# Staging the last x2 half of block 0 and the weight sums in the x region, and other queues and slots for loads and jobs

## The chip, the cores and the metric

One NeuronCore of one Trainium2 chip runs the kernel. The metric is the device time of one execution in microseconds (us). A profiled execution gives, beside its own time, the span from its first to its last recorded instruction, and the rows read below. TensorE is PE (its weight loads PEld), VectorE DVE, ScalarE ACT, GpSimd POOL and SyncE SP.

## What is computed

The reference chains a decaying causal attention and two feed-forward layers, over 8 x 576 = 4608 tokens and a width of 512:

```python
scores = scale * np.matmul(q, k.transpose(0, 1, 3, 2))
Dmat = np.where(rel >= 0, gamma[:, None, None] ** rel[None, :, :], 0.0)
x = np.matmul(scores * Dmat[None], v)          # to (4608, 512)
x2 = ((x @ w1) * (x @ w2)) @ w3 @ w_out        # d_ff 1024
h = x2 @ w_in                                  # d_ff 2048
out = (h * np.clip(h + 3.0, 0.0, 6.0) / 6.0) @ w_out2
```

The kernel multiplies in full precision by splitting each operand into a high and a low part (fp32r), with three matmuls for one product. It folds w3 @ w_out into one matrix W.

## The kernel before, in words

**Blocks.** The 4608 tokens are nine blocks (0 to 8) of 512. For each block PE computes, for the eight f-tiles of 128 of d_ff, `pa` = x @ w1 and `pb` = x @ w2 (lines 130 to 132, four tiles each of three matmuls for one k), then `px` = (a * b) @ W. Blocks 0 and 8 keep W whole in SBUF (`Wh`, `Wl`, `Wm`) and take `px` in 4 x 8 products of three matmuls. Blocks 1 to 7 take it in **seven products** of half size instead of eight (`px_str`, line 773: 168 matmuls of 256 columns): combinations of the halves of a * b (`pair`, `keep`) by combinations of the quarters of W, which stream from DRAM (`wsd`) through three buffers (`wb` in Wp's space, `st["w3"]` in the x region), 14 halves of 512 KB a block on SP (line 730). Four PSUM banks A to D gather the products; D is reused by the sixth product and C by the seventh, after VectorE's adds of line 748 have read them. Each block's result x2 is then turned into seven half-size operands as well (sums, high part, low part) and stored to DRAM (`xod`); so are the weights w_in (`wid`) and w_out2 (`wqd`), one "i" job and one "q" job in each of blocks 1 to 8 (`job`: load by SP at line 107, convert on ACT at line 155 and on DVE at lines 160 and 164, sums at line 861, high part at 864, low part at 135, store at 872; all in the one staging area `stg` and `stg_hi`). Stage 2 (h and the gate) and stage 3 (the last product) then read these operands back, with 896 to 1024 KB transfers; in stage 2, `stg` and `stg_hi` are the temporaries, and ACT's copy of line 1038 is the first step after a bank's first product.

**Attention in between.** At four places of a block PE makes an `excursion` (some 180 small matmuls, lines 214 and 251) that computes the attention of one 128-token tile t of a later block. It needs kv and qk of tile t+1, loaded by POOL (lines 193 and 198), and v scaled by DVE (`v_scale`, line 204).

**The order.** Everything is in program order per engine. `at(s, f)` puts a step at slot s, and each group of three large matmuls calls `tick()`, which emits the steps of the slot that is due:

```python
def at(s, f):
    slots.setdefault(max(s, now[0]), []).append(f)
def tick():
    q_ = slots.get(now[0], [])
    while q_:
        q_.pop(0)()
```

A slot thus sets where a step stands in its engine's row of instructions, not when it runs: an engine that is free runs ahead of PE, and a step that must wait holds up all that stand behind it on its engine. Block j begins at slot B0 + 96 j; its pa and pb take slots 0 to 63 and px slots 64 to 95.

**Around the end of block 0.** W's seven combinations are made from `Wh`, `Wl` and `Wm` by four weight jobs (`w_job`: sums at lines 593 and 597, high part on ACT at line 600, low part on DVE, two 512 KB stores at 607). They share two tiles in the space of block 0's x (`xh`, `xl`), so that a job's high part waits for the store before. Block 0's x2 comes out as px columns 0, 2, then 1, 3 (`x2_copy`, line 821): column 2 and column 3 are both copied into `stg[0:512]`, so that the copy of column 3 waits until the store of the first half (line 845) has read `stg`.

**Lines to follow.** 186 to 199 loads of qk and kv; 472 to 501 excursions and their loads; 587 to 617 weight jobs and the opening of the spaces that follow; 645 `a_copy` (frees the bank of pa); 673 to 693 the combinations of a * b in blocks 1 to 7; 738 to 764 the adds of px; 808 to 847 x2; 850 to 882 the i and q jobs; 936 to 947 the loads of the last block (`xop`, `wset`).

## Time and profile before

| | us |
|---|---|
| three runs, median (lowest to highest) | 1455.13 (1451.58 to 1455.41) |
| the profiled execution's own time | 1451.42 |
| its span | 1449.6 |
| PE busy | 1419.8 (98% of the span) |
| DVE busy | 1091.0 (75%) |
| ACT busy | 573.4 (40%) |
| POOL busy | 143.1 (10%) |
| mean DMA rate | 242 GB/s |

PE is busy but for 29.8 us. What is busy is no peak: a matmul at the lower of the clock's two levels counts as busy too. A saving can therefore come from PE's waits and from stretches at the lower clock, and each wait has a place, an engine that it waited for, and work that stood ahead on that engine. The span and the own time of the profiled execution differ by 1.8 us, which lies around the program.

### The profile page before, as it was taken

What the parts mean: (1) busy time and instruction counts of PE and PEld (TensorE: products, weight loads), DVE (VectorE), ACT (ScalarE), POOL (GpSimd) and SP (SyncE); (2) the same over time, 40 slices, a digit from 0 to 9 for tenths busy, and PEclk for the clock granted to TensorE, in tenths of its full rate; (3) what the DMA queues carried; (4) which work ended last, traced back from release to release, by engine and by line L of the source; (5) the groups of instructions that cost most, each with busy time, mean ns of one, the idle gap of its engine ahead of it and who ended that gap; (6) DMA issues with size and microseconds to landing.
All of it is one profiled execution on the core that took longest, in us unless ns stands there. A gap on an engine that the chain in (4) does not pass through costs nothing.

```text
span 1449.6 us, 28030 instructions
## 1 busy us (share of the span) xinstructions
PE 1419.8 (98%) x11315; PEld 1204.7 (83%) x11315; DVE 1091.0 (75%) x1880; ACT 573.4 (40%) x842; POOL 143.1 (10%) x329
## 2 busy tenths in 40 slices
PE   9999799999999999999799999999999999999999
PEld 4588688888888888889688898888888888888888
DVE  7888668786877777686436666665668899889897
ACT  7583334343434343333323343333334433433433
POOL 1101010100010101000002242221221000000000
PEclk9999899999999999999999999999999999999999
DMA  9775758787878787869999674645898444555441
GB/s 361 302 240 182 262 204 307 269 286 278 301 265 300 267 303 262 300 248 304 351 346 408 213 276 156 243 187 203 319 342 266 129 122 137 146 146 145 135 124 62
DMA packets 214658, 351.32 MB, mean 242 GB/s; under 512 B 11168, under 2 KB 144064, under 8 KB 210944
## 3 DMA queue, kind: packets, MB, share of 16 engines
q1 hardware_dynamic: 142432, 212.89, 43.1%
q0 software_dynamic: 21792, 73.72, 13.7%
q10 hardware_dynamic: 50304, 62.92, 12.3%
q8 instruction: 89, 1.46, 0.4%
q14 instruction: 41, 0.34, 0.1%
HBM read 231.51 MB, written 117.96 MB: 241 GB/s over the span
## 4 chain that ended last, share of the span: by engine, by line
PE 88%; DVE 6%; DMA 4%; ACT 1%; issue 1%; POOL 0%; ACTq 0%; DVEq 0%; POOLq 0%
PE pb L1299 16%; PE pb L130 12%; PE pb L132 12%; PE pb L131 12%; PE pb L1300 8%; PE px L773 6%; PE pa L130 4%; PE pa L131 4%; PE Wps L514 4%; PE pa L132 4%; PE z L251 2%; PE sc L214 2%; DMA wb<-wsd 1%; DMA xod<-wb 1%; DVE stg L135 1%; DVE pair L135 1%
## 5 line engine op out<-in xcount | busy, mean ns | idle before, releaser
L1299 PE MATMUL pb<-wq,op 128*128 128x512 f32 x1000 | 346.7, 391 | 0.0
L1300 PE MATMUL pb<-wq,op 128*128 128x256 f32 x1000 | 280.0, 280 | 0.0
L1299 PEld LDWEIGHTS pb<-wq,op 128*128 128x128 f32 x1000 | 187.0, 187 | 41.0
L130 PE MATMUL pb<-xop,wset 128*128 128x512 f32 (+1 forms) x558 | 205.3, 368 | 0.0
L131 PE MATMUL pb<-xop,wset 128*128 128x512 f32 (+1 forms) x558 | 205.2, 368 | 0.0
L132 PE MATMUL pb<-xop,wset 128*128 128x512 f32 (+1 forms) x558 | 205.2, 368 | 0.0
L1177 ACT CAST op<-unit 128x1024 fp32r<-128x1024 f32 x126 | 131.5, 1052 | 173.5 <-DVE unit L1163 152.8
L1300 PEld LDWEIGHTS pb<-wq,op 128*128 128x128 f32 x1000 | 189.0, 189 | 0.0
L135 DVE TENSOR_TENSOR op<-unit,op 128x1024 fp32r<-128x1024 f32 x126 | 154.0, 1222 | 30.5 <-ACT op L1177 30.5
L773 PE MATMUL px<-pair,wb 128*128 128x256 f32 x1176 | 147.6, 286 | 9.0 <-DVE x L748 4.8
L773 PEld LDWEIGHTS px<-pair,wb 128*128 128x128 f32 x1176 | 144.4, 193 | 11.6 <-issue 7.3
L132 PEld LDWEIGHTS pb<-xop,wset 128*128 128x128 f32 x558 | 105.2, 189 | 17.5
L131 PEld LDWEIGHTS pb<-xop,wset 128*128 128x128 f32 x558 | 105.2, 189 | 17.4
L130 PEld LDWEIGHTS pb<-xop,wset 128*128 128x128 f32 x558 | 105.2, 189 | 17.3
L130 PE MATMUL pa<-xh,w1h 128*128 128x512 f32 x280 | 111.3, 397 | 8.0 <-ACT a L645 8.0
L130 PE MATMUL pb<-xh,w2h 128*128 128x512 f32 x288 | 113.8, 395 | 0.0
L132 PE MATMUL pb<-xh,w2l 128*128 128x512 f32 x288 | 112.2, 390 | 0.0
L131 PE MATMUL pb<-xl,w2h 128*128 128x512 f32 x288 | 112.1, 389 | 0.0
L131 PE MATMUL pa<-xl,w1h 128*128 128x512 f32 x280 | 110.2, 394 | 0.0
L132 PE MATMUL pa<-xh,w1l 128*128 128x512 f32 x280 | 110.0, 393 | 0.0
L1163 DVE TENSOR_TENSOR unit<-unit 128x1024 f32<-128x1024 f32 x72 | 87.8, 1220 | 0.6
L684 ACT CAST pair<-sraw 128x512 fp32r<-128x512 f32 (+1 forms) x56 | 40.8, 728 | 95.6 <-DVE sraw L135 95.6
(204 smaller groups left out, 2231.6 us busy)
## 6 DMA issues: line engine op xcount, KB each, us to landing
wb<-wsd SPq DMA_DIRECT2D x98, 512.0 KB, 6.5
unit<-gd SPq DMA_DIRECT2D x72, 512.0 KB, 5.3
xop<-xod SPq DMA_DIRECT2D x28, 1024.0 KB, 7.7
xod<-wb ACTq DMA_DIRECT2D x28, 896.0 KB, 4.9
qk<-in_qk_dram POOLq DMA_DIRECT2D x36, 512.0 KB, 7.1
kv<-in_kv_dram POOLq DMA_DIRECT2D x32, 512.0 KB, 5.1
gd<-gw POOLq DMA_DIRECT2D x60, 256.0 KB, 2.7
gd<-g POOLq DMA_DIRECT2D x57, 256.0 KB, 3.7
```

Source lines behind the costliest of these rows:

```text
L130: nc.tensor.matmul(out=out_ap, lhsT=sh, rhs=mh, start=first, stop=False, **kw)
L131: nc.tensor.matmul(out=out_ap, lhsT=sh, rhs=ml, start=False, stop=False, **kw)
L132: nc.tensor.matmul(out=out_ap, lhsT=sl, rhs=mh, start=False, stop=last, **kw)
L135: eng.tensor_tensor(out=out_ap, in0=x, in1=y, op=ALU.subtract)
L214: nc.tensor.matmul(out=out_ap, lhsT=lhsT, rhs=rhs, start=True, stop=True, skip_group_check=True)
L514: nc.tensor.matmul(out=ps, lhsT=w3f[:, n // 4 % 8, n % 4 * 128:n % 4 * 128 + 128], rhs=wo[:, j, :], start=j == 0, stop=j == KF - 1)
L684: nc.scalar.copy(out=st["pair"][f % 4][:, 0, a:b], in_=st["raw"][:, a + 1:b + 1])
L773: nc.tensor.matmul(out=out_ap, lhsT=w[:, kk, x, ms], rhs=y, start=k not in seen, stop=kk == 3 and x == 1, skip_group_check=True)
L1163: nc.vector.tensor_tensor(out=f32_unit(o), in0=t[0], in1=t[1], op=f)
L1177: nc.scalar.copy(out=op_tiles(7 * b + p)[0], in_=src())
L1299: nc.tensor.matmul(out=c[k], lhsT=h[:, ts], rhs=w, start=first and kt == 0, stop=False, skip_group_check=True)
L1300: nc.tensor.matmul(out=c[k][:, 0:256], lhsT=l[:, ts], rhs=w[:, 0:256], start=False, stop=kt == 7, skip_group_check=True)
```

## The change

1. **x2 of block 0.** px columns 1 and 3 are copied into one new tile in the x region (`xl`), not into the pool `tmp` and into `stg`; the sums, high part, low part and store of that half come 11 slots later.
2. **Weight jobs.** Each of the four has one tile in turn (`xh`, `xl`, `xh`, `xl`) and keeps its high and low part in it; they stand at slots 65, 73, 97, 112 of block 0 (65, 73, 98, 106 before). `open_sw` comes 6 slots later.
3. **Late kv/qk loads.** The loads that follow the fourth excursion of blocks 1 to 6 (kv and qk for six tiles) are issued by SP, in its row behind the seven products' weights.
4. **Other slots.** The q jobs of blocks 1 to 7 load and convert 8 slots earlier and sum 4 slots later, with the store where it was; the first i job comes 8 slots later. In block 8 the i job comes 8 and the q job 16 slots later, the reload of `Wh` 6 slots later, and the `xop` loads 6 to 31 slots later (one stays).

```diff
-    def load_qk(t):
+    def load_qk(t, q=nc.gpsimd):
...
-        nc.gpsimd.dma_start(out=x.rearrange("p x b a i -> p (x b a i)"), in_=qk[2 * t:2 * t + 2].rearrange("g d x h i -> (g d) (x h i)"))
+        q.dma_start(out=x.rearrange("p x b a i -> p (x b a i)"), in_=qk[2 * t:2 * t + 2].rearrange("g d x h i -> (g d) (x h i)"))
...
-    def load_kv(t):
+    def load_kv(t, q=nc.gpsimd):
...
-        (nc.sync if t < 4 else nc.gpsimd).dma_start(out=y.rearrange("j g x n -> j g (x n)"), in_=kv[2 * t:2 * t + 2].rearrange("g j x h d -> j g (x h d)"))
+        (nc.sync if t < 4 else q).dma_start(out=y.rearrange("j g x n -> j g (x n)"), in_=kv[2 * t:2 * t + 2].rearrange("g j x h d -> j g (x h d)"))
...
-                    at(ex[t] + 1 + late, lambda i=i: load_kv(i))
+                    at(ex[t] + 1 + late, lambda i=i, q=nc.sync if late else nc.gpsimd: load_kv(i, q))
...
-                    at(ex[t] + 1 + late, lambda i=i: load_qk(i))
+                    at(ex[t] + 1 + late, lambda i=i, q=nc.sync if late else nc.gpsimd: load_qk(i, q))
...
-                if not q:
-                    st["w"] = [x_ps[0].tile([128, 2, 1024], F32, tag=t, name="wj") for t in ("xh", "xl")]
-                r = st["w"][0][:, 0].rearrange("p (o n) -> p o n", o=4)
+                st["w"] = w = x_ps[0].tile([128, 2, 1024], F32, tag=("xh", "xl")[q % 2], name="wj")
+                r, d = (w[:, i].rearrange("p (o n) -> p o n", o=4) for i in range(2))
...
             def hi():
-                nc.scalar.copy(out=st["w"][1][:, 1].bitcast(F32R), in_=st["w"][1][:, 0])
+                nc.scalar.copy(out=st["w"][:, 0].bitcast(F32R), in_=st["w"][:, 1])
...
-        for q, d in enumerate((65, 73, 98, 106)):
+        for q, d in enumerate((65, 73, 97, 112)):
             w_job(q, B0 + d)
...
-        at(B0 + SPB + 14, open_sw)
+        at(B0 + SPB * 1 + 20, open_sw)
...
                 if n > 1:
+                    s = now[0] + (11 if j == 0 and n == 3 else 0)
                     for d, f in enumerate((x2_sums, x2_hi, x2_lo)):
-                        at(now[0] + 1 + d, f)
-                    at(now[0] + 7, lambda n=n: x2_store(j, n - 2))
+                        at(s + 1 + d, f)
+                    at(s + 7, lambda n=n: x2_store(j, n - 2))
...
+            if j == 0 and n % 2:
+                if n == 1:
+                    st["x2"] = x_ps[0].tile([128, 2, 1024], F32, tag="xl", name="x2")
+                raw2[n // 2] = st["x2"][:, 0, 256 * n - 256:256 * n + 256]
             nc.scalar.copy(out=raw2[n // 2], in_=px)
...
-            for d, f in ((10, sums), (11, hi), (14, lo), (24 if key[0] == "q" and key[1] < NSET - 1 else 19, store)):
+            for d, f in zip((22, 23, 26, 32) if key[0] == "q" and key[1] < NSET - 1 else (10, 11, 14, 19), (sums, hi, lo, store)):
...
-            job(("i", n), (w_in2[n + NSET], w_in2[n]), A_SUMS, lambda hl, n=n: wid[n, hl], B0 + SPB * n + SPB + (20 if n < NSET - 1 else 12))
+            job(("i", n), (w_in2[n + NSET], w_in2[n]), A_SUMS, lambda hl, n=n: wid[n, hl], B0 + SPB * n + SPB + (28 if n == 0 else 20))
...
-                lambda hl, n=n: wqd[:, :, n, hl].rearrange("o p n -> p o n"), B0 + SPB * n + SPB + (70 if n < NSET - 1 else 32))
+                lambda hl, n=n: wqd[:, :, n, hl].rearrange("o p n -> p o n"), B0 + SPB * n + SPB + (62 if n < NSET - 1 else 48))
...
-        for i, s in enumerate((27, 58, 28, 29, 32, 38, 104)):
+        for i, s in enumerate((44, 72, 48, 54, 60, 66, 104)):
             at(E0 + s, lambda i=i: load_xop(0, i))
...
-        at(B0 + SPB * (STR[-1] + 1) + 24, lambda: w_again(False))
+        at(B0 + SPB * (STR[-1] + 1) + 30, lambda: w_again(False))
```

Three places show what this does to the rows of instructions (the number behind a name is that of its tile; after the change the lines below 587 have other numbers: 821 is 824, 645 is 643, 600 is 598, 748 is 747, 861 is 864).

ACT at the end of block 0, from the store of the first half of x2 on, before:

```order
L845 DMA xod0_66<-stghi_77 128x7x256
L845 DMA xod0_66<-stg_76 128x7x256
L821 COPY x2_1634<-px_1522 128x512
L821 COPY stg_76<-px_1632 128x512
L835 CAST stghi_77<-stg_76 128x512
L835 CAST stghi_77<-x2_1634 128x256
L835 CAST stghi_77<-stg_76 128x1024
L600 CAST wj_1366<-wj_1366 128x1024
L645 COPY a_1665<-pa_1660 128x512
```

and after:

```order
L848 DMA xod0_66<-stghi_77 128x7x256
L848 DMA xod0_66<-stg_76 128x7x256
L824 COPY x2_1635<-px_1522 128x512
L824 COPY x2_1635<-px_1632 128x512
L598 CAST wj_1666<-wj_1666 128x1024
L643 COPY a_1673<-pa_1661 128x512
L605 DMA wsd_74<-wj_1666 128x4x256 x2
L682 CAST pair_1698<-sraw_1702 128x512
L643 COPY a_1673<-pa_1711 128x512
L838 CAST stghi_77<-x2_1635 128x512
```

The second copy of px now goes to `x2_1635`, not to `stg`, and the three casts of x2 stand behind two copies of pa.

DVE in the px of block 3, from the last combination of `keep` to the last add of px, before:

```order
L160 SCALAR_TENSOR_TENSOR stg_76<-stg_76,sign_110 128x512
L164 SCALAR_TENSOR_TENSOR stg_76<-wr_3906,stg_76 128x512
L135 TENSOR_TENSOR pair_1708<-keep_1760,pair_1708 128x512
L135 TENSOR_TENSOR pair_1759<-keep_1760,pair_1759 128x512
L748 TENSOR_TENSOR x1_3914<-x1_3914,px_3918 128x2x256
L861 TENSOR_TENSOR stg_76<-stg_76 128x256 x4
L748 TENSOR_TENSOR x1_3914<-x1_3914,px_3919 128x2x256
L748 TENSOR_TENSOR x1_3914<-x1_3914,px_3917 128x2x256
L135 TENSOR_TENSOR stg_76<-stg_76,stghi_77 128x1792
```

and after:

```order
L135 TENSOR_TENSOR pair_1699<-keep_1789,pair_1699 128x512
L135 TENSOR_TENSOR pair_1700<-keep_1789,pair_1700 128x512
L135 TENSOR_TENSOR pair_1788<-keep_1789,pair_1788 128x512
L747 TENSOR_TENSOR x1_3919<-x1_3919,px_3923 128x2x256
L747 TENSOR_TENSOR x1_3919<-x1_3919,px_3924 128x2x256
L747 TENSOR_TENSOR x1_3919<-x1_3919,px_3922 128x2x256
L864 TENSOR_TENSOR stg_76<-stg_76 128x256 x4
L135 TENSOR_TENSOR stg_76<-stg_76,stghi_77 128x1792
```

The q job's conversions (line 160 and 164) now stand ahead of the fourth excursion, and its sums behind the adds that free banks D and C.

SP in block 8, from the second i load on, before:

```order
L107 DMA wr_7595<-in_w_in2_dram 128x512
L107 DMA wr_7685<-in_w_out2_dram 128x512
L107 DMA wr_7711<-in_w_out2_dram 128x512
L585 DMA Wh_7724<-wsd_74 128x4x256 x4
L925 DMA xop_7745<-xod0_66 128x2048
```

and after:

```order
L107 DMA wr_7613<-in_w_in2_dram 128x512
L107 DMA wr_7634<-in_w_in2_dram 128x512
L585 DMA Wh_7749<-wsd_74 128x4x256 x4
L107 DMA wr_7782<-in_w_out2_dram 128x512
L107 DMA wr_7801<-in_w_out2_dram 128x512
L928 DMA xop_7822<-xod0_66 128x2048
```

The q job's two loads now stand behind the reload of `Wh`, and the `xop` loads still follow directly.

## Rows read from the trace of the kernel before

**Rows 1.** PE's waits by what ended them: total us, times, longest

```profile
PE px L773 <- DVE x L748: 4.8, 3, 1.9
PE px L773 <- DMA wb<-wsd: 2.7, 2, 1.6
...
PE px L773 <- issue: 1.3, 1, 1.3
```

**Rows 2.** Timeline of PE: start, length in us, instruction, [idle before <-what ended it]

```profile
152.19 0.39 PE L131 MATMUL pb<-xl,w2h 128*128 128x512 f32 x1
152.41 0.39 PE L132 MATMUL pb<-xh,w2l 128*128 128x512 f32 x1
...
172.28 1.13 PE L214 MATMUL sc<-kv 64*64 64x64 f32 x32 [7.28 <-DVE kv L204]
...
717.12 0.80 PE L130 MATMUL pa<-xh,w1h 128*128 128x512 f32 x1 [7.95 <-ACT a L645]
```

**Rows 3.** Two stretches: busy of five engines, granted clock, DMA share, GB/s

```profile
172.28:178.00 5.72, 5.72 (x59) 4.74 (x60) 5.58 (x13) 2.61 (x5) 1.28 (x2) 0.57 0.55 186
717.12:721.00 3.88, 3.88 (x11) 3.14 (x12) 3.58 (x8) 1.42 (x2) 0.10 (x1) 0.63 1.03 427
```

**Rows 4.** Timeline of ACT, end of block 0 and start of block 1

```profile
150.79 0.59 ACT L821 COPY stg<-px 128x512 f32<-128x512 f32 x1 [6.77 <-DMA xod<-stg]
...
164.22 1.04 ACT L600 CAST wj<-wj 128x1024 fp32r<-128x1024 f32 x1 [3.32 <-DMA wsd<-wj]
```

**Rows 5.** Timeline of DVE, end of block 0 and start of block 1

```profile
136.40 0.41 DVE L135 TENSOR_TENSOR stg<-x 128x256 f32<-128x256 f32 x1
...
139.12 1.22 DVE L135 TENSOR_TENSOR stg<-stg,stghi 128x1024 fp32r<-128x1024 f32 x1
...
152.42 0.68 DVE L593 TENSOR_TENSOR wj<-Wh,Wl 128x512 f32<-128x512 f32 x1
...
153.74 1.56 DVE L597 TENSOR_TENSOR wj<-wj 128x256 f32<-128x256 f32 x4
...
167.21 1.23 DVE L135 TENSOR_TENSOR wj<-wj 128x1024 fp32r<-128x1024 f32 x1 [4.25 <-DMA wsd<-wj]
...
169.69 0.41 DVE L135 TENSOR_TENSOR keep<-sraw 128x256 f32<-128x256 f32 x1
```

**Rows 6.** Timeline of DVE, px of block 3

```profile
368.27 0.69 DVE L160 SCALAR_TENSOR_TENSOR stg<-stg,sign 128x512 int32<-128x512 int32 x1
...
371.40 1.55 DVE L861 TENSOR_TENSOR stg<-stg 128x256 f32<-128x256 f32 x4
372.87 1.40 DVE L748 TENSOR_TENSOR x<-x,px 128x512 f32<-128x512 f32 x2
```

**Rows 7.** Timelines of SP and POOL, px of block 1

```profile
206.95 14.31 SPq L730 DMA_DIRECT2D wb<-wsd  x10
...
214.69 0.71 POOL L198 DMA_DIRECT2D kv<-in_kv_dram  x1 [1.41 <-PE z L251]
```

**Rows 8.** DMA issues from 206 to 224: transfer, queue, count, size, median us to landing

```profile
wb<-wsd SPq DMA_DIRECT2D x10, 512.0 KB, 6.7
```

**Rows 9.** DMA issues from 653 to 672, px of block 7

```profile
wb<-wsd SPq DMA_DIRECT2D x10, 512.0 KB, 5.0
wqd<-stghi ACTq DMA_DIRECT2D x1, 896.0 KB, 4.9
```

**Rows 10.** Timelines of ACT and SP, block 8

```profile
712.66 0.66 ACT L155 ACTIVATE stg<-wr 128x512 f32<-128x512 f32 x1 [10.29 <-DMA wid<-stg]
...
743.58 0.59 ACT L821 COPY stg<-px 128x512 f32<-128x512 f32 x1 [3.02 <-DMA wqd<-stg]
...
746.41 0.37 SPq L845 DMA_DIRECT2D xod<-stghi  x1
```

**Rows 11.** DMA issues from 725 to 729, the q job's store in block 8

```profile
wqd<-stg ACTq DMA_DIRECT2D x1, 896.0 KB, 18.4
```

**Rows 12.** DMA issues from 746 to 747, the store of x2 in block 8

```profile
xod<-stghi SPq DMA_DIRECT2D x1, 896.0 KB, 5.6
```

More of the change, by code (lines that the diff above doesn't have):

```diff
@@ L588, in sums @@
             def sums():
-                if not q:
-                    st["w"] = [x_ps[0].tile([128, 2, 1024], F32, tag=t, name="wj") for t in ("xh", "xl")]
-                r = st["w"][0][:, 0].rearrange("p (o n) -> p o n", o=4)
+                st["w"] = w = x_ps[0].tile([128, 2, 1024], F32, tag=("xh", "xl")[q % 2], name="wj")
+                r, d = (w[:, i].rearrange("p (o n) -> p o n", o=4) for i in range(2))
                 for i, f in enumerate((q, q + 4)):
-                    nc.vector.tensor_tensor(out=st["w"][0][:, 0, 512 * i:512 * i + 512], in0=Wh[:, f].bitcast(F32), in1=Wl(f).bitcast(F32), op=ALU.add)
-                d = st["w"][1][:, 0].rearrange("p (o n) -> p o n", o=4)
+                    nc.vector.tensor_tensor(out=w[:, 0, 512 * i:512 * i + 512], in0=Wh[:, f].bitcast(F32), in1=Wl(f).bitcast(F32), op=ALU.add)
                 a11, a21, a12, a22 = (r[:, i] for i in range(4))
@@ L599, in hi @@
             def hi():
-                nc.scalar.copy(out=st["w"][1][:, 1].bitcast(F32R), in_=st["w"][1][:, 0])
+                nc.scalar.copy(out=st["w"][:, 0].bitcast(F32R), in_=st["w"][:, 1])
             def lo():
-                sub(nc.vector, st["w"][0][:, 1].bitcast(F32R), st["w"][1][:, 0], st["w"][1][:, 1].bitcast(F32R))
+                sub(nc.vector, st["w"][:, 1].bitcast(F32R), st["w"][:, 1], st["w"][:, 0].bitcast(F32R))
             def store():
-                for hl, t in enumerate((st["w"][1], st["w"][0])):
-                    nc.scalar.dma_start(out=wsd[4:8, q, :, hl].rearrange("o p n -> p o n"), in_=t[:, 1].rearrange("p (o n) -> p o n", o=4))
+                for hl in range(2):
+                    nc.scalar.dma_start(out=wsd[4:8, q, :, hl].rearrange("o p n -> p o n"), in_=st["w"][:, hl].rearrange("p (o n) -> p o n", o=4))
             for d, f in ((0, sums), (2, hi), (3, lo), (6, store)):
@@ L612, in retention_moe_kernel @@
         at(B0 + 44, w_quads)
-        for q, d in enumerate((65, 73, 98, 106)):
+        for q, d in enumerate((65, 73, 97, 112)):
             w_job(q, B0 + d)
-        at(B0 + SPB + 1, open_a)
-        at(B0 + SPB + 6, open_st)
-        at(B0 + SPB + 14, open_sw)
+        at(B0 + SPB * 1 + 1, open_a)
+        at(B0 + SPB * 1 + 6, open_st)
+        at(B0 + SPB * 1 + 20, open_sw)
         def ffn1(j):
```

## The prediction

> **What bounds the kernel now.** I read the waits of PE first, since PE is busy for 1419.8 of 1449.6 us. Its idle 29.8 us are few and large. In the timeline of PE, one wait of 7.28 us ends at 172.28, in block 1, and one of 7.95 us at 717.12, in block 8 [rows 2]; six waits of 1.1 to 1.9 us, one in the px of each of blocks 1 to 6, add up to 4.8 + 2.7 + 1.3 = 8.8 us [rows 1]. The reader is to see that 24 of the 29.8 us are in these eight places, and that the change touches the work in front of each. A long wait costs twice: the granted clock of the stretch behind the first has a mean of 0.57 over 5.72 us, behind the second 0.63 over 3.88 us [rows 3], so the lower of the two levels (1.2 of 2.4 GHz) holds for a while after PE starts again. That loses 0.43 x 5.72 = 2.5 us and 0.37 x 3.88 = 1.4 us. Three matmuls, one slot, take 0.683 us (starts 0.22 to 0.23 apart, [rows 2]).
>
> **Block 1, before.** The chain that ends the first wait starts with a store: ACT's copy of px column 3 into `stg` waits 6.77 us for the store of the first x2 half [rows 4]. ACT's later casts and DVE behind it are late by that; then the fourth weight job's high part on ACT waits 3.32 us for the third job's store [rows 4], its low part on DVE 4.25 us [rows 5], and v's scaling, on which PE waits, stands behind both.
>
> **Block 1, after.** Both waits lose their cause: column 3 goes into another tile, and jobs 1 to 4 take `xh`, `xl`, `xh`, `xl`. Job 3 so overwrites the tile of job 1, and job 4 that of the x2 half, which had followed job 2; what reads those tiles is long done. No store is left in front of v's scaling; the work itself is. I add it up in the new order of DVE. Block 1's first `pb` ends at 152.41 + 0.39 = 152.8 [rows 2]; its combination, high part and low part end near 155.3 (0.68 + 0.42 + 0.62 + 0.69 and some 0.1, an estimate from like instructions of rows 4 and 5). Then x2's sums and low parts, 136.40 to 140.34, so 3.9 us; then the weight job's sums, 152.42 to 155.30, so 2.9; then the combinations of the next f-tile, from 167.21 + 1.23 = 168.4 to 169.69 + 0.41 = 170.1, so 1.7 [rows 5]. That is 163.8. From there to PE's start it took 172.28 - 170.1 = 2.2 us before; now ACT's cast of the weight job (1.04, [rows 4]) and DVE's low part (1.2, [rows 5]) stand in between: 163.8 + 2.2 + 1.0 + 1.2 = **168.2**. PE arrives at 172.28 - 7.28 = 165.0. A wait of 3.2 us remains: **gain 4.1**. Bounds: none gone if DVE falls as far behind as before (0), all gone if the casts overlap better (7.3). The loss by the clock, 2.5, need not go: a 3.2 us wait may bring the lower level again. I take 1.0 of 2.5. Next late there is the weight job's last store, in front of the low part of x of block 2; it is issued near 167 and is needed near 175, and DVE's next scaling of v has some 0.5 us to spare; I take nothing for it and keep 1 us in the range.
>
> **px of blocks 1 to 6.** Two causes. (a) DVE: the q job's sums (1.55 us) stand between the first add and the two adds that free bank D, and four converts of 0.7 each stand a little ahead [rows 6]. After the change the converts stand ahead of the excursion, where DVE waits for PE anyway, and the sums behind the adds. That moves 1.55 + 4 x 0.6 = 4.0 us away from the front of adds that were late by at most 1.9: the 4.8 and the "issue" 1.3 go. The sums are then late by one add's distance, but the next add is needed only at the next product's end; nothing else waits for them until the store. (b) DMA: POOL is not paced by slots; it issues the "late" kv and qk (1 MB) at 214.69, right behind its fence, in the middle of the weight stream, which SP issues from 206.95 to 221.26 [rows 7]. On SP these loads stand behind the last weight half. In this px a weight half needs 6.7 us to land [rows 8], in block 7, where no such loads exist, 5.0 [rows 9], and there PE has no wait: the 2.7 go too. On SP the i job's two loads move behind 1 MB more, some 3 us; they were issued some 10 us ahead of the block's end and are needed 20 slots (13.7 us) after it. POOL loses twelve loads and gains nothing by it. Bounds: 8.8 and, if (b) fails, 6.1. I take **8.3**, leaving 0.5 for what may newly show.
>
> By the Trainium skill ("DMA: Bandwidth & Descriptors", Issuing engines are not separate DMA queues), transfers from SP, ACT and GpSimd run on the same 16 DMA engines and interleave, whoever issues them. By that rule alone moving kv and qk to SP would not take a byte from the stream, and (b) would give 0. I side with the rows, since here the moved loads also start later.
>
> **Block 8, before.** ACT's convert for the q job waits until 712.66 for the i job's store, which still reads `stg` [rows 10]; behind it stands the copy that frees a bank of pa, and PE waits 7.95 us [rows 2].
>
> **Block 8, after.** The q job's loads are behind the reload of `Wh`, so that its convert can hardly start before 712 either; but 16 slots later in ACT's row, two more copies of pa stand in front of it, and the bank behind it is needed only at px, 12 slots (8.2 us) after PE's old stop at 717.12 - 7.95 = 709.2, thus at 717.4 plus the 4 slots of the tile between, 720. **Gain 7.95 + 1.4 = 9.35**, and stage 2 starts at 717.12 + 48 x 0.683 + 1.4 = 751.3 - 9.35 = 741.9. `xop` moves in the row, but SP is not paced by slots: it issues those loads right behind the q loads, as before near 705.
>
> **What is late next.** The q job's store does not move with PE. Before, it needed 18.4 us to land [rows 11], since the `xop` and weight sets fill the DMA engines, and ACT's copy of px column 2 waited for it until 743.58 [rows 10]; that was 7.7 us ahead of stage 2. The store is now issued at the same time within 1 us (the job starts as late, near 712). So the copy comes at 743.6 to 745, now behind the start of stage 2. From it to the first store of x2 it took 746.41 - 743.58 = 2.8 us [rows 10], to that store's landing 5.6 [rows 12], and only then may stage 2's first copy overwrite `stg_hi`: 752.0 to 753.4, done 0.6 later. PE needs it when it takes up the first bank again, 12 slots after its start: 741.9 + 8.2 = 750.1. A **new wait of 2.5 to 4 us**; I take 3.3. Bounds: 0, if the store lands as it did in block 7 (4.9, [rows 9]), and 6 with the clock's fall. Net gain of block 8: 9.35 - 3.3 = **6.0**.
>
> The Trainium skill (the same page, Queues, rings and completion order) says that each DMA engine takes turns between the queues, a packet at a time. By that alone 1.8 MB on ACT's queue would get half of the engines, some 9 us by the 427 GB/s of rows 3, and the new wait would not be there (the second rival); the 18.4 us of rows 11 speak against it.
>
> **Sum.** 4.1 + 1.0 + 8.3 + 6.0 = 19.4 us of the profiled execution's 1451.4: **1432.0**. That execution is 3.7 us below the median of the runs shown (1455.1) and 0.2 below the fastest; I don't add this, and keep it for the range.
>
> **Rivals.**
> - *No new wait in stage 2* (chance 0.2). For it: the store's 18.4 us hold only while SP's loads are queued. Against it: they are still queued. 1432.0 - 3.3, and a cleaner block 1 by up to 3: 1426 to 1429.
> - *The loads' queue makes no difference* (0.12): the weight stream still waits in px, by the rule above; for it, DMA is near full in px in any case; against it, rows 9. 1432.0 + 2.7 = 1434.7.
> - *Stage 2 starves* (0.08): the same bytes have to be in 9 us earlier, and sets 0 and 1 land only then. For it: a DMA share of 1.03 [rows 3]. Against it: by my count of the bytes the sets land 2 us ahead. With 8 us more: 1440.
> - *SP is held up by the new loads* (0.04, the slower side): kv on SP waits for its buffer; behind it stand the i job's loads, and ACT's converts wait for those, with PE's banks behind ACT, as in block 8. Place: the start of blocks 2 to 7. It decides when SP loses more than some 14 us there (10 us of lead and 13.7 to the need, less 9 to land). Each us beyond costs 6; with 5 us, 30 - 19.4: 1462. Against it: the buffer is read for the last time in the fourth excursion, which ended before POOL's issue at 214.69 [rows 7].
> - The forecast, with a new wait of 2.5 to 4 us, has 0.52; the 0.04 left are for gains that are lost to something no row here shows, with a time near the old one.
>
> **How the numbers follow.** The range takes in the first three rivals and both ends of the clock's loss, and the 3.7 us by which runs stand above the profiled one: 1425 to 1441. About 0.3% (4.4 us) is what a measurement of this kernel can tell from no change. Above 1455.1 - 4.4 = 1450.7 lie only the slow rival, 0.04, and the 0.04 left over: faster 0.92, the same 0.04, slower 0.04.
>
> **What would show it.** Right: PE's wait in front of `sc<-kv` near 168 instead of 172, with no store in DVE's or ACT's waits ahead of it; in px of blocks 1 to 6 no wait over 0.5 us; kv and qk on SP's queue behind the weight halves; no wait near 709; a wait of some 3 us of the first bank of stage 2 near 750, ended by ACT's copy. Wrong: waits of over 1 us in px, a wait for weights (`wset` or `xop`) at the start of stage 2, or ACT's converts waiting for loads at the start of blocks 2 to 7.

## The result, and the profile after

The changed kernel takes 1438.46 us in the median (1437.82 to 1438.98, four runs), beside 1453.64 us for the kernel before (1451.58 to 1455.41): a ratio of 0.9899, 95% interval 0.9882 to 0.9916. It is 15.2 us faster. The forecast was 1432.0 in a range of 1425 to 1441. The direction and the range hold; 6.5 us are missing. The profiled execution took 1437.82 us, with a span of 1436.0, so 13.6 us less than the span before.

PE is busy for 1420.0 us, as before (1419.8); its idle time fell from 29.8 to 16.0 us. The waits of PE by what ended them, in the changed kernel (total us, times, longest):

```profile
PE sc L214 <- DVE kv L204: 4.2, 2, 3.0
PE pb L130 <- ACT x2l L824: 3.0, 1, 3.0
PE px L130 <- ACT a L643: 2.9, 1, 2.9
```

All waits of px in blocks 1 to 6 [rows 1] are gone. In place of the two long waits [rows 2] there are four shorter ones. Timeline of PE in the changed kernel (start, length, instruction, [idle before <- what ended it]); the row at 730.97 is the first of stage 2:

```profile
168.38 0.90 PE L214 MATMUL sc<-kv 64*64 64x64 f32 x32 [2.97 <-DVE kv L204]
...
183.58 0.69 PE L214 MATMUL sc<-kv 64*64 64x64 f32 x32 [1.21 <-DVE kv L204]
...
707.48 0.50 PE L130 MATMUL px<-abh,Wh 128*128 128x512 f32 x1 [2.93 <-ACT a L643]
...
730.97 0.39 PE L130 MATMUL pb<-xop,wset 128*128 128x512 f32 x1
...
739.62 0.79 PE L130 MATMUL pb<-xop,wset 128*128 128x512 f32 x1 [3.04 <-ACT x2l L824]
```

Behind three of them the granted clock is low, as it was behind the two of before [rows 3]. Stretches of the changed kernel (length, busy of PE, PEld, DVE, ACT, POOL, granted clock, DMA share, GB/s):

```profile
168.38:174.00 5.62, 5.62 (x62) 4.69 (x63) 4.04 (x10) 1.29 (x3) 1.28 (x2) 0.70 1.08 380
...
707.48:711.00 3.52, 3.52 (x9) 2.79 (x10) 3.45 (x8) 1.07 (x2) 0.10 (x1) 0.58 1.01 424
711.00:714.00 3.00, 3.00 (x14) 2.42 (x13) 1.85 (x2) 1.72 (x2) 0.00 (x0) 0.93 1.03 433
...
739.62:743.00 3.38, 3.38 (x8) 2.70 (x9) 3.17 (x7) 2.33 (x4) 0.00 (x0) 0.50 1.03 340
743.00:746.00 3.00, 3.00 (x9) 2.33 (x9) 2.34 (x5) 0.70 (x2) 0.00 (x0) 0.57 1.02 332
```

The clock took 0.30 x 5.62 = 1.7 us in block 1, 0.42 x 3.52 + 0.07 x 3.00 = 1.7 us in px of block 8, and 0.50 x 3.38 + 0.43 x 3.00 = 3.0 us at the start of stage 2.

Where the 13.6 us come from is best read from starts of PE's rows in both traces, cut at the same instructions. Blocks begin where the first `pa` of a block follows px, and a px begins at its first matmul:

| stretch of PE | before, us | after, us | gain | forecast |
|---|---|---|---|---|
| to the start of block 1 | 147.20 | 147.60 | -0.4 | 0 |
| `pa`, `pb` and excursions of block 1 | 59.79 | 56.32 | 3.5 | 5.1 |
| px of blocks 1 to 7, summed | 168.22 | 155.80 | 12.4 | 8.3 |
| `pa`, `pb` and excursions of blocks 2 to 7, summed | 301.13 | 301.13 | 0 | 0 |
| block 8, to the start of stage 2 | 74.90 | 70.12 | 4.8 | 9.35 |
| stages 2 and 3, to the end of the span | 698.36 | 705.03 | -6.7 | -3.3 |
| sum | 1449.6 | 1436.0 | 13.6 | 19.4 |

So block 1 came short by 1.6, px brought 4.1 more, and the end of block 8 with the start of stage 2, forecast as a gain of 6.0, is a loss of 1.9 in these two traces. That last place is where most runs below went.

Each column is one execution. Ten of the kernels below have the same steps in block 1 as the changed kernel, and there that stretch took 54.9 to 58.4 us; three (`u_queue`, `u_qjob`, `u_stage`) have the same steps from block 8 on, and there the last two stretches together took 774.5 to 776.7 us, for 775.2 here and 773.3 before. So a difference of some 2 us in one such stretch is not clear of this scatter. The seven px scatter less: without the edits that touch them they sum to 155.7 to 156.7.

### The profile page after: what moved, and what is told of

Same layout as the page of the kernel before. It is cut to its first block, busy times and chain, and to the rows that moved or that the text cites. A ratio compares the mean times of both kernels' runs of the same rounds, so it can differ in the third digit from the quotient of the medians.

```text
span 1436.0 us, 28035 instructions
## 1 busy us (share of the span) xinstructions
PE 1420.0 (99%) x11315; PEld 1205.0 (84%) x11315; DVE 1091.2 (76%) x1880; ACT 572.8 (40%) x842; POOL 135.5 (9%) x317
## 3 DMA queue, kind: packets, MB, share of 16 engines
q0 software_dynamic: 20064, 67.43, 12.4%
## 4 chain that ended last, share of the span: by engine, by line
PE 93%; DMA 4%; DVE 2%; ACT 1%; issue 1%; POOL 0%; ACTq 0%; DVEq 0%; POOLq 0%
PE pb L1302 16%; PE pb L130 12%; PE pb L132 12%; PE pb L131 12%; PE px L772 10%; PE pb L1303 8%; PE Wps L514 4%; PE pa L130 4%; PE pa L131 4%; PE pa L132 4%; PE z L251 3%; PE sc L214 2%; DMA wqd<-stg 1%; DMA wsd<-wj 1%; DMA xod<-wb 1%; DMA wid<-stg 1%
## 5 line engine op out<-in xcount | busy, mean ns | idle before, releaser
L772 PE MATMUL px<-pair,wb 128*128 128x256 f32 x1176 | 144.1, 284 | 0.0
L979 DVE TENSOR_TENSOR stghi<-stghi,pb 128x256 f32<-128x256 f32 (+1 forms) x128 | 61.3, 479 | 21.1 <-PE pb L132 19.6
```

The costliest lines, as they stand in the source:

```text
L772: nc.tensor.matmul(out=out_ap, lhsT=w[:, kk, x, ms], rhs=y, start=k not in seen, stop=kk == 3 and x == 1, skip_group_check=True)
L979: nc.vector.tensor_tensor(out=out_ap, in0=a, in1=b, op=ALU.add)
```

## The experiments

Twelve kernels in four groups. The first four take one part of the change back; the others are the changed kernel with something added in block 8. The kernel before ran beside every one of them and took 1451.2 to 1453.5 us in the median; the changed kernel has only the four runs above, so that some 2 us between two medians say little, and the stretch that an edit touches is read in the trace as well.

### One part undone at a time

**`u_block8`.** Block 8's slots as before:

```diff
-... B0 + SPB * n + SPB + (28 if n == 0 else 20))
+... B0 + SPB * n + SPB + (28 if n == 0 else 20 if n < NSET - 1 else 12))
-... (62 if n < NSET - 1 else 48))
+... (62 if n < NSET - 1 else 32))
-for i, s in enumerate((44, 72, 48, 54, 60, 66, 104)):
+for i, s in enumerate((27, 58, 28, 29, 32, 38, 104)):
-at(B0 + SPB * (STR[-1] + 1) + 30, lambda: w_again(False))
+at(B0 + SPB * (STR[-1] + 1) + 24, lambda: w_again(False))
```

> The changed kernel with block 8's slots as before (i job 12, q job 32, xop 27 to 104, reload of Wh 24). From the trace of the changed kernel, theory A: block 8 and the start of stage 2 gave nothing back, because the wait of 7.95 us was exchanged for one of 2.93 in px and one of 3.04 in stage 2, each with a clock fall behind it (1.7 and 3.0 us lost, against 1.4 before). Without this part the 8 us wait in front of pa is back near 702, the other two are gone, and the time is 1.5 to 2.5 us lower than the changed kernel's 1438.5: 1436 to 1437. Theory B (the prediction's step): this part is worth 6.0 us, so without it 1444.5. No difference within 0.5 us would speak for neither.

Measured: 1438.34 us (1437.61 to 1439.39), the time of the changed kernel within 0.1. The old wait is back, and neither of the two new ones is there. Its timeline of PE:

```profile
702.58 0.79 PE L130 MATMUL pa<-xh,w1h 128*128 128x512 f32 x1 [8.33 <-ACT a L643]
```

The prediction's step (6.0 us) falls. My first theory from the trace, that this part costs 2 us, falls as well: from the start of block 8 on, this kernel takes 774.5 us, the changed one 775.2. What was exchanged has the same price: one wait of 8.3 us with 2.0 lost by the clock behind it (0.50 over 3.42 us, 0.93 over the next 4.00), for waits of 2.9 and 3.0 us with 1.7 and 3.0.

**`u_queue`.** The late kv and qk on POOL again:

```diff
-... q=nc.sync if late else nc.gpsimd: load_kv(i, q))
+... q=nc.gpsimd: load_kv(i, q))
```

(and the same for `load_qk`).

> The changed kernel with the late kv and qk loads issued by POOL again. Theory A (the loads in the middle of the weight stream delay it): PE waits for wb are back in px of blocks 1 and 2, some 2.7 us, weight halves land in over 6 us there; 1441 to 1442.5. Theory B (whoever issues them, the bytes share the same DMA engines, and the waits were due to the q job's work on DVE alone): no wait for wb over 0.3 us, 1438.5 within 0.5.

Measured: 1444.72 us (1443.26 to 1450.65), 6.3 more than the changed kernel. In the waits of PE, six for weights are back, and the DMA issues of 203 to 222 show the halves landing in 7.1 us:

```profile
PE px L772 <- DMA wb<-wsd: 4.7, 6, 1.9
```

```profile
wb<-wsd SPq DMA_DIRECT2D x10, 512.0 KB, 7.1
```

In the changed kernel the same issues land in 5.3:

```profile
wb<-wsd SPq DMA_DIRECT2D x10, 512.0 KB, 5.3
```

The rival "the loads' queue makes no difference" is refuted for the move as it was made. The trace speaks for order in time as the reason, and not for the queue as such; no run has the loads on POOL but later, which would part the two. POOL issues kv at 211.53 in this kernel, in the middle of the weight stream, SP at 218.38 in the changed one, behind it. In the timelines of POOL in `u_queue` and of SP in the changed kernel:

```profile
211.53 0.71 POOL L198 DMA_DIRECT2D kv<-in_kv_dram  x1 [1.41 <-PE z L251]
```

```profile
203.89 14.31 SPq L729 DMA_DIRECT2D wb<-wsd  x10
218.38 0.37 SPq L198 DMA_DIRECT2D kv<-in_kv_dram  x1
```

The px of blocks 1 to 7 sum to 162.2 us here, for 155.8: all of the 6.3 us lies in them. Of it 4.7 are these waits; the rest is 0.2 to 0.5 us in each of the five px that have such a wait, and no row names it. The wait at the start of stage 2 is longer in this profile (5.5 us), but from block 8 on it takes 775.4 us, for 775.2.

**`u_qjob`.** The q jobs of blocks 1 to 7 at their old slots:

```diff
-... (62 if n < NSET - 1 else 48))
+... (70 if n < NSET - 1 else 48))
-... zip((22, 23, 26, 32) if key[0] == "q" and key[1] < NSET - 1 else (10, 11, 14, 19), (sums, hi, lo, store)):
+... zip((10, 11, 14, 24) if key[0] == "q" and key[1] < NSET - 1 else (10, 11, 14, 19), (sums, hi, lo, store)):
```

> The changed kernel with the q jobs of blocks 1 to 7 at their old slots (load and convert 8 slots later, sums 4 slots earlier relative to the block). Theory A (sums and converts on DVE stand in front of the adds that free banks D and C): waits of 1.3 to 2 us for DVE L747 are back in px of four blocks or more, and the clock falls behind the longest of them; 6 to 8 us more, 1444.5 to 1446.5. Theory B (the adds were late because the weights were late, so that the SP queue alone takes the waits away): under 2 us more, below 1440.5.

Measured: 1448.14 us (1445.43 to 1451.68), 9.7 more. Six waits in px are back, as long as before the change although the late loads are on SP. Waits of PE, and DVE in px of block 1, where the sums (L864) stand between the adds (L747) again:

```profile
PE px L772 <- issue: 8.9, 6, 2.0
```

```profile
218.21 0.68 DVE L747 TENSOR_TENSOR x<-x,px 128x512 f32<-128x512 f32 x1
218.81 1.55 DVE L864 TENSOR_TENSOR stg<-stg 128x256 f32<-128x256 f32 x4
220.28 1.40 DVE L747 TENSOR_TENSOR x<-x,px 128x512 f32<-128x512 f32 x2
```

PE starts again at 221.06, while the two adds behind the sums run. So the two causes in px were not two shares of one sum. The q job alone keeps every one of the six waits (8.9 of 8.8 us); the loads alone keep 4.7. They ran beside each other, and the longer one showed. By the whole time of the seven px it is the same: 168.1 us with the q job undone, as before the change (168.2), and 162.2 with the loads undone. Moving the loads without the q job would have won nothing in px, and the q job without the loads 4.1 us of the 8.8 in waits, 6.0 of the 12.4 in time.

**`u_stage`.** Block 0's x2, the four weight jobs and their slots as before (parts 1 and 2 of the change taken back, the slot of `open_sw` with them):

```diff
-... enumerate((65, 73, 97, 112)):
+... enumerate((65, 73, 98, 106)):
...
-s = now[0] + (11 if j == 0 and n == 3 else 0)
+s = now[0]
```

> The changed kernel with block 0's x2 and the weight jobs staged as before and at their old slots. Theory A: the wait in front of v's scaling in block 1 is back at about 7 us instead of 2.97, and the 1.21 us wait of the next excursion is gone; net 3.5 us more (the measured gain of block 1): 1442. Theory B (part of block 1's gain came from elsewhere, as from the first i job's later slot): 1439 to 1440.5 with a wait below 6 us.

Measured: 1441.70 us (1440.46 to 1443.09), 3.2 more. The long wait is back, and the one of 1.21 us behind it is gone, as theory A has it; `pa`, `pb` and excursions of block 1 take 60.3 us, for 56.3. Timeline of PE:

```profile
172.42 1.13 PE L214 MATMUL sc<-kv 64*64 64x64 f32 x32 [7.11 <-DVE kv L204]
```

Undone one at a time, the four parts cost 0 + 6.3 + 9.7 + 3.2 = 19.2 us, more than the 15.2 that all of them bring: the loads and the q job hide each other. The later slot of the first i job was not undone by itself; `u_stage` has it, and its long wait is 7.11 us for 7.28 before.

### Block 8: one wait taken away at a time

**`q60`.** The q job of block 8 stands 12 slots later, so that two more copies of pa are ahead of its converts on ACT:

```diff
-... (62 if n < NSET - 1 else 48))
+... (62 if n < NSET - 1 else 60))
```

> The changed kernel with block 8's q job 12 slots later (60 for 48): on ACT two more copies of pa stand in front of its converts. Theory A: the wait of 2.93 us at the start of block 8's px goes, and the clock loss of 1.7 behind it, but the q job's store lands at the same time within 1 us (735.5), so that the wait of stage 2, behind ACT's copy of px column 2, grows by as much: 6 to 8 us there and no net change, 1437.5 to 1439.5. Theory B: the store is issued and lands as much earlier as PE is, and 4 us are won: 1433.5 to 1435.

Measured: 1438.47 us (1438.05 to 1439.53): nothing gained. The wait in px is gone, and the one in stage 2 grew from 3.04 to 7.47. Timelines of PE and ACT:

```profile
740.58 0.79 PE L130 MATMUL pb<-xop,wset 128*128 128x512 f32 x1 [7.47 <-ACT x2l L824]
```

```profile
736.51 0.58 ACT L824 COPY stg<-px 128x512 f32<-128x512 f32 x1 [17.21 <-DMA wqd<-stg]
739.45 0.58 ACT L824 COPY x<-px 128x512 f32<-128x512 f32 x1
739.93 0.59 ACT L824 COPY x2l<-px 128x512 f32<-128x512 f32 x1
```

PE stands for the q job's store in either case. The copy that waits for it comes at 736.5, beside 735.55 in the changed kernel, and PE's earlier start is given back whole.

**`x2a`.** The first x2 half of block 8 gets a tile of its own, so that no copy of px waits for the store; weight set 2, which comes into that space, is loaded later:

```diff
-                if j == NB - 1 and n % 2:
-                    x2l = wab_p.tile([128, 2, 2048], F32, tag="B2", name="x2l")
+                if j == NB - 1:
+                    x2l = wab_p.tile([128, 2, 2048], F32, tag="B2" if n % 2 else "A2", name="x2l" if n % 2 else "x2a")
...
-... ("A2", 80) ...
+... ("A2", 103) ...
```

(with ACT's one-element write in `load_set(2)` left out).

> The changed kernel with block 8's first x2 half in a tile of its own (in the space of w2's high part), and not in stg; weight set 2, which takes that space, is loaded at slot 103 of block 8 for 80. Theory A: ACT's copy of px column 2 no longer waits for the q job's store; the wait of 3.04 us in stage 2 and the clock loss of 3.0 behind it go, and the first copy of stage 2 into stghi finds its store landed (733 against 736): 1431.5 to 1433.5. Theory B: set 2 or xop now comes late, a wait of 1 to 3 us for one of them within 20 us after the start of stage 2: 1434 to 1437. Theory C: the wait only moves to the first copy into stghi: 1438.

Measured: 1442.46 us (1440.70 to 1444.91), 4 us more than the changed kernel. The wait for `x2l` is gone, and 12 us later another stands in its place:

```profile
751.35 0.77 PE L130 MATMUL pb<-xop,wset 128*128 128x512 f32 x1 [4.54 <-DMA xop<-xod]
```

Theory B by kind, with a larger price. The last `xop` load stands on SP behind set 2 and behind the stores of x2.

**`x2a_q60`.** Both edits.

> Both of the two edits. Theory A: no wait in px of block 8 either, 4.6 us less than x2a: 1427 to 1429.5. Theory B: stage 2 then starts near 726, ahead of the landing of the q job's store in stghi or of xop and set 1, and 2 to 4 us of wait and clock loss are given back: 1430 to 1433.

Measured: 1440.34 us (1439.36 to 1440.90). The wait in px is gone, and the one for `xop` is 10.05 us. Of the 4.6 us that px gives, 2.1 are left against `x2a`, and the time is above theory B's range.

### Who sets the time of the store

**`s2`.** One slot: weight set 2 is loaded at 97 of block 8, behind the stores of the first x2 half on SP:

```diff
-... ("A2", 80) ...
+... ("A2", 97) ...
```

> The changed kernel with one slot moved: weight set 2 of stage 2 (1.8 MB, first used some 18 us after the start of stage 2) is loaded at slot 97 of block 8 for 80, so that its load stands behind the stores of the first x2 half. Theory A (the q job's store lands only when the bytes that SP has queued beside it have drained, 420 GB/s full): without these 1.8 MB it lands some 4 us earlier, near 731 for 735.5; ACT's copy of px column 2 comes with it, the wait of 3.04 us in stage 2 shrinks below 0.5, and set 2 and xop 6 still come in time: 1432 to 1434. Theory B: the store's time does not hang on set 2 (it was issued after the store), landing within 1.5 us of 735.5, 1437.5 to 1439.5. Theory C: the wait goes, but set 2 or xop 6 comes 1 to 4 us late: 1435 to 1439 with a wait for DMA in stage 2.

Measured: 1443.05 us (1442.11 to 1444.42), theory C at twice its price, and theory A's first half to the point. The DMA issues of 715 to 716, in the changed kernel and in this one:

```profile
wqd<-stghi ACTq DMA_DIRECT2D x1, 896.0 KB, 18.3
wqd<-stg ACTq DMA_DIRECT2D x1, 896.0 KB, 20.1
```

```profile
wqd<-stghi ACTq DMA_DIRECT2D x1, 896.0 KB, 12.9
wqd<-stg ACTq DMA_DIRECT2D x1, 896.0 KB, 15.0
```

The store lands 5.1 us earlier (1.8 MB at some 420 GB/s are 4.4), though set 2's load was issued after it (at 720.31 in the changed kernel). PE's wait for ACT is gone. But now set 2 and the x2 stores stand ahead of the last `xop` load, and PE waits 8.74 us for that:

```profile
757.45 0.77 PE L130 MATMUL pb<-xop,wset 128*128 128x512 f32 x1 [8.74 <-DMA xop<-xod]
```

**`pool`.** The low parts of block 8's two jobs are stored from POOL's queue:

```diff
-                    nc.scalar.dma_start(out=o, ...
+                    (nc.gpsimd if hl and key[1] == NSET - 1 else nc.scalar).dma_start(out=o, ...
```

> The changed kernel with the low parts of block 8's i and q jobs stored from POOL's queue, the high parts from ACT's as before. Theory A (a queue's share of the DMA engines is what limits these stores): the low parts land in under 13 us for the q job (20.1 before) and under 9 for the i job (11.2), the waits of 2.93 and 3.04 us shrink to under 1.5 each, 1431 to 1435. Theory B (the engines are full, the bytes decide): landings within 2 us of what they were, 1437.5 to 1439.5.

Measured: 1436.70 us (1434.12 to 1437.58), 1.8 less than the changed kernel, with a ratio of 0.9889 (0.9871 to 0.9907) that is not clear of that kernel's. From block 8 on its trace takes 772.5 us, for 775.2. The low part lands in 12.5 us, but the high part on ACT in 20.7, and ACT's cast into `stghi` waits for that one instead; PE's waits are 1.82 and 3.62 us. The queue is not all that differs: SP issues set 1 at 713.81 here, 1.1 us behind POOL's store, and at 707.02 in the changed kernel. What its queues carried from 716 to 725 (packets, MB, share of the engines; q1 is SP, q0 POOL, q10 ACT), and the q job's stores:

```profile
q1 hardware_dynamic: 320, 2.04, 54.1%
q0 software_dynamic: 240, 0.92, 25.1%
q10 hardware_dynamic: 740, 0.75, 23.6%
```

```profile
wqd<-stg POOLq DMA_DIRECT2D x1, 896.0 KB, 12.5
wqd<-stghi ACTq DMA_DIRECT2D x1, 896.0 KB, 20.7
```

**`pool2`.** Both parts on POOL's queue (`hl and` left out of the line above).

> As the run with low parts on POOL's queue, but with both parts of block 8's i and q jobs there. Theory A (POOL's queue is served faster than ACT's beside SP's loads: 12.5 us for one 896 KB store against 20.7): both parts of the q job land within 17 us of their issue, the high part some 4 us earlier than 733.5, and the wait of 3.62 us in stage 2 goes below 1.5; 1430 to 1433. Theory B (the two stores share what POOL's queue gets): both land at 18 to 22 us, and the time is that of the run with one part, 1436.7, or that of the changed kernel, 1438.5.

Measured: 1442.95 us (1438.95 to 1443.93). Both stores of the q job land in about 7 us, and the median is 4.5 us above the changed kernel's all the same:

```profile
wqd<-stghi POOLq DMA_DIRECT2D x1, 896.0 KB, 7.1
wqd<-stg POOLq DMA_DIRECT2D x1, 896.0 KB, 6.6
```

```profile
724.53 0.94 SPq L904 DMA_DIRECT2D wset<-wid  x2
```

The last row, of SP, shows what it cost. POOL also writes one element of each of these tiles ahead of its load; those writes now stand in POOL's row behind a store that waits for its data, so that set 1 is loaded at 724.53, for 707.02 in the changed kernel. The engines then carried 219 GB/s from 720 to 730, and the stores had them nearly to themselves: the first moved 0.89 of its 0.92 MB from 719 to 723.2, with SP's queue at 6% of the engines. But the loads were late, the first x2 store met them (11.7 us to land), and PE waited 2.45 us for that and 3.89 us at px. Neither expectation had thought of it.

That this is why the kernel is slower is not shown. The profiled execution is the fastest of the four (1438.95 us); from block 8 on it takes 774.0 us, for 775.2 in the changed kernel. It has 2.1 us more in block 1, whose steps are the same. The other three runs took some 4 us longer, and no trace shows where. What the run does show is the price of the store with little of SP's queue beside it: 7 us, not 20.

### Towards a faster kernel

**`late8`.** `pool`, and in block 8 the sums, high and low part and store of the first x2 half come behind the copy of the last px column, the change's own remedy for block 0 (the tile of `a` takes column 1; `kept` holds the tiles of each half until then, in two more lines that are not shown):

```diff
+                    if j == NB - 1:
+                        s = E0 + SPB
+                        for d, f in ((1, x2_sums), (2, x2_hi), (3, x2_lo), (7, lambda n=n: x2_store(j, n - 2))):
+                            at(s + d, lambda f=f, n=n: (raw2.update(kept[n][0]), x2b.update(kept[n][1]), f()))
+                        continue
...
-                raw2[0] = pools["tmp"].tile([128, BLK1], F32, tag="x2", name="x2", bufs=1)
+                raw2[0] = pools["tmp"].tile([128, BLK1], F32, tag="a" if j == NB - 1 and n else "x2", name="x2", bufs=1)
```

> The run with low parts on POOL's queue, and in block 8 the sums, high part, low part and store of the first x2 half put behind the copy of the last px column (slots 97 to 103), as the change does it in block 0; column 1 is copied into the tile of a, so that no copy of px waits for the first half. Theory A: no bank of px is held by ACT's wait for the q job's store, so the wait for ACT x2l goes; stage 2 runs on until it needs its temporaries in stghi (x2's store, landing near 739 to 741), and 0 to 2 us of wait are left there: 1431 to 1434. Theory B: all of it only moves behind L1041's copy into stghi, or to xop 6, whose load waits for the x2 stores: 1436 to 1439.

Measured: 1435.70 us (1435.16 to 1436.22), between the two expectations; from block 8 on it takes 773.1 us. All four copies of px come in time, and PE runs on until stage 2 needs `stghi`:

```profile
741.57 0.79 PE L130 MATMUL pb<-xop,wset 128*128 128x512 f32 x1 [4.99 <-ACT stghi L1049]
```

This is the wait that the prediction had named (the copy of line 1038 before, 1049 in this kernel): PE stops 8.3 us after the start of stage 2 (728.26 to 736.58), 12 slots, where it stopped after 5.6 in the changed kernel.

**`late8s2`.** The same with set 2 at slot 97.

> The kernel late8 (low parts on POOL's queue, first x2 half of block 8 behind the last px column) with set 2 at slot 97 as well. Theory A: the high part of the q job lands near 730.5 for 734.7, the first x2 store near 738 for 740.9, and the wait of 4.99 us for the copy into stghi goes to 1 to 3: 1431 to 1434. Theory B: no change against late8's 1435.7 within 1. Theory C: set 2 or xop 6 late, 1436 to 1439.

Measured: 1432.80 us (1431.76 to 1436.41), a ratio of 0.9878 (0.9860 to 0.9897) to the kernel before. It is the lowest median of all, 5.7 us below the changed kernel; all four runs lie below that kernel's four, though the intervals of the two ratios overlap. Between the two profiled spans there are 5.7 us as well: 4.0 of them from block 8 on (771.1 for 775.2), 1.4 in block 1, which has the same steps. Set 2's load, ahead of the x2 stores here, is issued at 727.13 (717.61 in `late8`) and so all but keeps out of the q job's store. Its high part lands in 16.2 us, for 20.9. The wait in stage 2, from the waits of PE, is now

```profile
PE pb L130 <- ACT stghi L1049: 3.9, 1, 3.9
```

The same slot that cost 4.6 us by itself (5.0 from block 8 on) won 2.0 from block 8 on here (773.1 to 771.1). The 2.9 between the medians are not clear of the scatter: one of the four runs took 1436.41, and block 1 took 2.4 us less in this profile than in that of `late8`. The x2 halves are ready earlier, the last `xop` load is issued at 737.46, for 740.11 in `s2`, lands in 11.4 us, and PE does not wait for it.

## Why the prediction was right, and where it missed

**Block 1: right, the clock not.** The working by DVE's row gave 168.2 for PE's start and a rest of 3.2 us; measured were 168.38 and 2.97. No store stands ahead of v's scaling any more. Two sizes were off. Of the clock's 2.5 us I took 1.0 back; the loss is still 1.7 behind the shorter wait, so 0.8 came back. And the weight job's last store, for which "I take nothing", costs 1.21 us: DVE's low part of x of block 2 waits for it, and with it the next scaling of v (L204). Timeline of DVE after:

```profile
165.63 1.23 DVE L135 TENSOR_TENSOR wj<-wj 128x1024 fp32r<-128x1024 f32 x1 [1.51 <-ACT wj L598]
...
167.64 0.69 DVE L204 TENSOR_TENSOR kv<-kv,rate 128x512 f32<-128x512 f32 x1
...
179.24 0.69 DVE L135 TENSOR_TENSOR xl<-x,xh 128x512 fp32r<-128x512 f32 x1 [6.36 <-DMA wsd<-wj]
```

That makes 4.3 + 0.8 - 1.2 = 3.9; the table's 3.5 leaves 0.4 that no row names. The 1.21 is the size in this one execution: in the profiles below with the same steps that wait is absent (`pool`, `late8s2`) to 2.29 us long (`late8`).

**px: right in both causes, wrong in their sum.** All 8.8 us of waits went, as forecast, where 8.3 was taken. The step that failed is the split into 6.1 for the q job and 2.7 for the loads. `u_qjob` and `u_queue` show waits of 8.9 and 4.7, side by side. And I had not looked at the clock behind the longest wait in px, 1.95 us [rows 1]. Stretches of the kernel before:

```profile
298.07:302.00 3.93, 3.93 (x32) 3.93 (x33) 3.46 (x5) 2.17 (x2) 0.00 (x0) 1.00 1.05 406
...
596.48:600.00 3.52, 3.52 (x19) 3.52 (x20) 2.64 (x2) 1.51 (x2) 0.00 (x0) 0.59 1.04 398
600.00:604.00 4.00, 4.00 (x32) 3.98 (x32) 0.71 (x2) 0.62 (x1) 0.00 (x0) 0.94 1.08 387
```

Behind the 1.64 us wait of block 2 the clock stays up (first row); behind the 1.95 it falls. That is 0.41 x 3.52 + 0.06 x 4.00 = 1.7 us more, and px of block 6 gained 25.78 - 22.13 = 3.65 us, not 1.95. The remaining 1.9 of the 12.4 lie as 0.0 to 0.6 us in each of the seven px and are named by no row; with the q jobs at their old slots (`u_qjob`) they are back too.

**Block 8: the cause right, the time of the store and the path of the wait wrong.** The wait near 709 of the old trace is gone, and a wait of "some 3 us" at the start of stage 2, behind ACT's copy of px column 2 and the q job's store, is there at 3.04. To compare times, 15.5 us (676.34 - 660.85, the two starts of block 8) are added to those of the changed kernel. The first step that failed is that the store is "issued at the same time within 1 us": it is issued at 715.36 + 15.5 = 730.9, for 725.06 before. The i job, too, had been moved by 8 slots, and I had priced only the q job's move. Its store is issued later, 691.69 + 15.5 = 707.2 for 703.46, and takes 11.2 us to land. So the q job's convert starts not near 712 but at 703.01 + 15.5 = 718.5. ACT in the changed kernel, where the copy that frees PE's bank stands behind the converts:

```profile
703.01 0.66 ACT L155 ACTIVATE stg<-wr 128x512 f32<-128x512 f32 x1 [8.78 <-DMA wid<-stg]
...
706.87 0.56 ACT L643 COPY a<-pa 128x512 f32<-128x512 f32 x1
...
735.55 0.59 ACT L824 COPY stg<-px 128x512 f32<-128x512 f32 x1 [15.26 <-DMA wqd<-stg]
...
738.98 0.59 ACT L824 COPY x2l<-px 128x512 f32<-128x512 f32 x1
...
742.62 0.59 ACT L1041 COPY stghi<-pb 128x512 f32<-128x512 f32 x1 [0.40 <-PE pb L132]
```

PE needs that bank at 704.55, thus at 720.0 of the old time, as forecast; the copy is late by 2.93 us. This wait was not in the sum.

The second is the path of the new wait. The forecast had PE stop 8.2 us (12 slots) after the start of stage 2, until x2's first store had landed and the copy of line 1038 had gone into `stg_hi`: 2.8 + 5.6 + 0.6 us behind the copy of px column 2. In the trace PE stops 5.6 us after that start (730.97 to 736.58), and what it waits for is ACT's copy of the last px column, 3.4 us behind that of column 2 (735.55 to 738.98). The copy into `stg_hi`, line 1041 here, comes later, at 742.62, and PE does not wait for it. Its row names PE, but the product that it reads had long been done (in the kernel before, the same copy runs 2.9 us after the start of stage 2); what came last was x2's first store, issued at 738.38 and landed 4.2 us later. In old time PE stopped at 752.1 for 750.1 and went on at 755.1 for 752.6 to 754.0; that both ends slipped alike is luck, and so is the size of 3.04 for 3.3. The wait that was forecast is what PE meets in `pool2`, `late8` and `late8s2`.

The chain of waits from 700 to 745 says it in one line: the two stores are 70% of it.

```profile
by line: DMA wqd<-stg 44.7%; DMA wid<-stg 25.0%; issue 8.0%; DVE stg L135 4.9%; PE pb L130 4.6%; PE pb L131 3.8%; PE pb L132 3.8%; ACT stghi L867 3.8%; ACT raw L156 3.3%; DVE stg L864 3.2%; DVE stg L160 3.1%; DVE ab L658 3.0%; ACT abh L662 
```

The other term is the clock. I had counted 1.4 us back in block 8 and nothing lost behind the new wait; in fact 1.7 and 3.0 us are lost behind two. In block 8 the 1.4 did not come back and 0.3 more went; with the wait of 2.93 these are the 4.6 by which 9.35 was too much. In stage 2 the wait is 3.0 for 3.3, and the clock's 3.0 with 0.7 that no row names make 6.7. The bound of 6 "with the clock's fall" was nearer than the value taken.

**The total.** That it stayed in the range is in part luck: against the forecast the first stretch, block 1 and the end of block 8 with stage 2 gave 0.4, 1.6 and 7.9 us less, and px, whose price was wrong too, gave 4.1 more.

**Rivals.** No new wait in stage 2 (0.2), the first of the list, which the prediction's text calls the second: did not happen. The queue makes no difference (0.12): refuted by `u_queue`, for queue and time of issue together. Stage 2 starves (0.08): not in the changed kernel, but it is what stands next, as `x2a`, `x2a_q60` and `s2` show with waits of 4.5 to 10 us for `xop`. SP held up by the new loads (0.04): PE has no wait at the start of blocks 2 to 7, which take the same 301.13 us as before.

## What to carry to other kernels

When a staging buffer is handed from a store to the next step, the time to look up is when the store lands, not when the engine reaches the step; where SP keeps the DMA engines full, that time goes with the bytes queued, so every job moved ahead of it must be priced, and a step that only moves along the engine's row moves the wait with it. Two causes in front of the same wait are not to be split into shares: take the longer one away and the other appears at its own size. To each wait add what the granted clock of the stretch behind it shows: here 1.7 to 3.0 us behind waits of 1.95 to 3.04 us. And compare two kernels in the stretch that the edit touches: block 1, untouched, differed by 2.4 us between the profiles of `late8` and `late8s2`.

## What the runs showed of the hardware

**A store's landing beside a busy queue.** The q job's 896 KB take 18 to 21 us from ACT's queue while SP's loads are queued, 15.0 with 1.8 MB less of them (`s2`), and 6.6 to 7.1 where SP's loads were held back (`pool2`, from POOL's queue, so that two things differ). What the queues carried from 716 to 733 in the changed kernel (packets, MB, share of the engines):

```profile
q1 hardware_dynamic: 809, 5.32, 74.7%
q10 hardware_dynamic: 1625, 1.65, 27.3%
```

SP's packets are 5.32 MB / 809 = 6.6 KB, ACT's 1.0 KB. ACT had twice as many packets and 27.3% of the engines' time, for SP's 74.7%. The Trainium skill ("DMA: Bandwidth & Descriptors", Queues, rings and completion order) has the engines take turns a packet at a time; from that I had worked out half of the bytes for each queue. These rows show that neither the packets nor the bytes were shared evenly; whether what the profile counts as a packet is what that page calls one, no run here shows. Over the life of the q job's store (issued at 714.94 and 715.36, landed at 735.5) the shares change:

| from to, us | SP: MB, share of the engines | ACT: MB, share of the engines |
|---|---|---|
| 715.4 to 719 | 1.48, 99.0% | 0.03, 2.3% |
| 719 to 727 | 2.91, 86.3% | 0.44, 15.6% |
| 727 to 735.5 | 1.19, 33.7% | 1.36, 45.3% |

So the store moved three quarters of its 1.8 MB in its last 8.5 us, when SP's queue took a third of the engines.

**The same tile from POOL's queue goes in larger packets.** In `pool` they are 0.92 MB / 240 = 3.8 KB, beside ACT's 1.0 KB, and `stg` lands in 12.5 us, for 20.1 from ACT's queue in the changed kernel (and for 20.7 of `stghi` beside it). SP's loads beside it are not the same as there, since set 1 is issued 6.8 us later.

**The clock behind short waits.** In the kernel before it stayed at the upper of its two levels (1.00) behind the five px waits of 1.1 to 1.6 us and went to a mean of 0.59 over 3.52 us behind the one of 1.95. I had looked for the lower level (1.2 of 2.4 GHz) only behind the two long waits. The length of the wait alone does not settle it: behind 1.88 us (px of block 1 in `u_queue`) and 1.89 us (block 1 in `q60`) the clock stayed at 1.00, behind 1.83 us (block 1 in `pool2`) it had a mean of 0.71 over 3.08 us.
